# Attention and a gated feed-forward in one kernel: token blocks of 384 become blocks of 512, with a first pass laid out anew

## The chip, the core and the metric

The kernel runs on one NeuronCore of a Trainium2 chip. TensorE (PE in the profile; its weight loads are PEld) multiplies 128x128 stationary weights by a moving operand and adds into PSUM, eight banks of 128 x 2 KB. VectorE (DVE) and ScalarE (ACT) do elementwise work, GpSimd (POOL) a little of it and one DMA queue, SyncE (SP) issues nearly all DMAs. The metric is the device time of one launch in microseconds (us).

## What is computed

```python
# q, k, v: (8, 8, 576, 64) float32
pool = 8
scale = 1.0 / np.sqrt(D)
k_p = k.reshape(B, H, Sp, pool, D).mean(axis=3)
v_p = v.reshape(B, H, Sp, pool, D).mean(axis=3)
scores = scale * np.matmul(q, k_p.transpose(0, 1, 3, 2))
scores = scores - np.max(scores, axis=-1, keepdims=True)
attn = np.exp(scores)
attn = attn / (np.sum(attn, axis=-1, keepdims=True) + 1e-09)
return np.matmul(attn, v_p).astype(np.float32)
...
# x: (4608, 512) from the heads; w_gate, w_val: (512, 1536) float64; w_out: (1536, 512) float64
gate = 1.0 / (1.0 + np.exp(-(x @ w_gate)))
val = x @ w_val
return (gate * val @ w_out).astype(np.float32)
```

Keys and values are averaged in groups of eight, so each query sees 72 keys. The 4,608 rows of `x` are called tokens below. Nearly all multiplications lie in the three products with the weights.

## The kernel before

**Precision.** A float32 operand of the three products is split in a high part, a copy rounded to TensorE's float32r, and a low part, the rest. A product is then three matmuls: high x high, high x low, low x high. ACT writes the high part and DVE subtracts to get the low one (`split`, L173 to 176). The weights arrive as float64 words; `to_f32` (L191) makes float32 of them in four instructions, two on ACT and two on DVE.

**Blocks.** The tokens are cut into `NB` = 12 blocks of `BT` = 384. A matmul of the first two products ("chain") moves 384 columns, one block. A batch has 576 tokens, so a block can touch two batches; `segments` cuts it there.

**Passes.** `first_pass` (L878) takes blocks 0 and 1 plainly: for each of 12 chunks `f` of the hidden width, `whole` (L658) makes gate and value with 12 matmuls each, and `accumulate` (L1153) makes the third product with 128x512 matmuls. Meanwhile it loads and converts every weight (`converted`, `converted_o`, `summed_o`), writes the split parts to DRAM for later (`keep_parts`, `keep_whole`, `keep_o`, `keep_sums`), and does the attention of blocks 0 to 3. Its instructions stand on every engine in the order of the words of `ORDER` (L67): for instance `conv.0.3` is one more step of converting the gate weights of pair 3, `G.1.5` a product, `lw` a load of weights, `acc.4.0` a step of the third product.

Then five passes take two blocks each, with seven products in place of eight by sums of blocks (Winograd's form): `hidden` (L713) walks six pairs `p` of chunks through `SLOTS`, 14 products of 6 matmuls each (`product`, L618; the matmul is L627), and `second_sums` (L809) does the third product with 21 units (m, q) of 12 matmuls (L844). So a pass has 504 + 252 matmuls. Between them one step at a time of the attention of the next pass's blocks is put in (`attention`, L485, a generator; `tasks`). The last pass has none. In the first of the five, pass 1, chunks 10 and 11 go plainly (`hidden_second`, L687: 96 matmuls, L667), and only five pairs follow, whose parts are partly new: `add_up` (L257) makes the sums of the quarters of a weight on DVE, and `reload(..., fresh=True)` splits one part of each group (L175, L176) and stores it from POOL's queue.

**Order.** In the passes a scheduler orders each engine's instructions by estimated due times, apart from those held in program order; engines are in order when they run.

**Rooms in SBUF.** Tags name the rooms: `big` (4 rooms of 8 KB per partition: raw weights, sums, the third product's operands `hs`), `parts` (8 of 4 KB: weight parts of the chain), `oparts` (4 of 4 KB: parts of `w_out`), `xo1` to `xo7` (the split parts of x). In the third product `reload_s` (L364) fetches the parts of unit i+2 and `operand` (L793) splits its `hs` while unit i runs, both into rings of four.

**PSUM.** Six banks `b0` to `b5` hold chains and third products, `sc` and `tp` attention. The scores of a block and a pair of heads are 3 x 144 columns, one bank; `reduce_max` (L506), a subtraction (L509) and one exponential over two pairs (L514) follow. In blocks 0 to 3 the exponential reads PSUM with the maximum as its bias, six instructions of 72 columns (L983). After a product with m = 1, 5 or 6, ACT copies the bank (L633) before the next product may add to it.

## Time and profile before

| | us |
|---|---|
| median of 3 runs (959.38 to 962.64) | 962.57 |
| the profiled execution, its own time | 963.26 |
| its span, first to last instruction | 961.5 |
| first pass, to the last 128x512 matmul of its third product | 215.7 |
| pass 1, to its last third-product matmul | 160.1 |
| passes 2, 3, 4 | 150.7, 150.6, 151.0 |
| pass 5 (no attention beside it) | 129.7 |
| last stores | 3.7 |

The stages are read from the trace by the first and last start of the third product's matmuls (L1159 in the first pass, 252 of L844 in each later one). Busy time of an engine is the union of its instructions; a matmul's recorded duration, 334 ns for 384 columns, holds its way through the array, so the distance from start to start is what one costs in a stream.

### The profile page before, as it was taken

Reading aid. Unit: us, or ns where it says so; the run is one execution under the profiler, and the core shown is the slowest. Engines: PE = TensorE matmul, PEld = TensorE weight load, DVE = VectorE, ACT = ScalarE, POOL = GpSimd, SP = SyncE. Lnnn points to the kernel's source line nnn. Section 1 sums busy time; section 2 is a strip of 40 time slices with the busy share of each in tenths; the row PEclk is TensorE's granted clock in tenths of the full one; section 3 lists DMA queues with packets and bytes.
Section 4 is the critical chain, followed back from the end, with each engine's and each line's share of the span. In section 5 each row is a group of like instructions: output and inputs, shape, how many; then the busy total and the mean of one; then the engine's idle time right before and its main releaser. Section 6 shows DMA issues by size and latency. Waiting matters only on the chain.

```text
span 961.5 us, 15330 instructions
## 1 busy us (share of the span) xinstructions
PE 931.8 (97%) x5400; PEld 901.3 (94%) x5400; DVE 680.7 (71%) x1207; ACT 554.9 (58%) x1142; POOL 70.0 (7%) x107
## 2 busy tenths in 40 slices
PE   4899999999999999999999999999999999999998
PEld 4799998889999999999999999999999999999997
DVE  6987777768888897767586566688476678344483
ACT  6998865544666576656554456655456556233352
POOL 1200000001332100000000000000000000000000
PEclk9999999999999999999999999999999999999999
DMA  9998967779977478988378867568877548877476
GB/s 306 379 294 313 343 228 253 252 257 342 324 259 232 138 238 294 373 312 255 120 226 275 277 228 249 177 200 256 300 254 243 179 121 262 287 233 247 153 221 217
DMA packets 107324, 243.23 MB, mean 253 GB/s; under 512 B 11376, under 2 KB 45936, under 8 KB 105712
## 3 DMA queue, kind: packets, MB, share of 16 engines
q1 hardware_dynamic: 104048, 231.77, 72.6%
q0 software_dynamic: 3200, 10.49, 2.8%
q8 instruction: 43, 0.70, 0.3%
q14 instruction: 33, 0.27, 0.1%
HBM read 191.88 MB, written 50.33 MB: 252 GB/s over the span
## 4 chain that ended last, share of the span: by engine, by line
PE 69%; DMA 7%; DVE 3%; ACT 1%; issue 1%; SPq 0%; DVEq 0%; ACTq 0%
PE chain L627 37%; PE acc L844 21%; PE sc L460 3%; PE chain L667 2%; PE av L469 2%; PE acc L1159 2%; DMA out<-o 1%; DMA raw<-in_kT 1%; PE tp L548 1%; DMA oparts<-keptS 1%; DMA w<-keptwV 1%; DMA raw_o<-in_wo 0%; DMA parts<-keptV2B 0%; DMA oparts<-keptO 0%; DMA parts<-keptV3B 0%
## 5 line engine op out<-in xcount | busy, mean ns | idle before, releaser
L627 PE MATMUL chain<-xo,parts 128*128 128x384 f32 x2436 | 453.7, 338 | 5.7 <-DVE y L639 1.7
L627 PEld LDWEIGHTS chain<-xo,parts 128*128 128x128 f32 x2436 | 419.8, 188 | 10.3 <-issue 2.8
L844 PE MATMUL acc<-hs,oparts 128*128 128x384 f32 x1260 | 227.7, 335 | 1.8 <-ACT hs L803 0.5
L844 PEld LDWEIGHTS acc<-hs,oparts 128*128 128x128 f32 x1260 | 218.3, 188 | 3.6 <-issue 2.3
L639 DVE TENSOR_TENSOR y<-chain,sG 128x384 f32<-128x384 f32 x87 | 48.0, 552 | 67.8 <-ACT sG L633 26.5
L667 PE MATMUL chain<-xo,parts 128*128 128x384 f32 x504 | 93.2, 339 | 0.0
L667 PEld LDWEIGHTS chain<-xo,parts 128*128 128x128 f32 x504 | 88.4, 190 | 0.3
L639 DVE TENSOR_TENSOR y<-chain,sV 128x384 f32<-128x384 f32 x87 | 47.9, 552 | 47.2 <-PE chain L627 32.4
L645 ACT ACTIVATE gate<-y 128x384 f32<-128x384 f32 x87 | 45.6, 525 | 54.4 <-DVE y L639 54.0
L633 ACT COPY sV<-chain 128x384 f32<-128x384 f32 x87 | 41.1, 477 | 53.7 <-PE chain L627 35.9
L803 ACT CAST hs<-h 128x768 fp32r<-128x768 f32 x60 | 50.2, 837 | 32.8 <-PE acc L844 30.2
L633 ACT COPY sG<-chain 128x384 f32<-128x384 f32 x87 | 41.2, 476 | 42.3 <-PE chain L627 42.1
L804 DVE TENSOR_TENSOR hs<-h,hs 128x768 fp32r<-128x768 f32 x60 | 56.7, 953 | 12.4 <-ACT hs L803 12.3
L542 POOL TENSOR_TENSOR pm<-e,rz 128x384 f32<-128x384 f32 x32 | 28.7, 895 | 441.0 <-DVE r L482 223.6
L803 ACT CAST hs<-s 128x768 fp32r<-128x768 f32 x45 | 37.3, 837 | 27.9 <-PE acc L844 19.8
L1159 PE MATMUL acc<-oparts,hs 128*128 128x512 f32 x216 | 51.8, 393 | 0.2 <-DVE hs L1149 0.2
L460 PE MATMUL sc<-kbd,raw 128*128 128x144 f32 (+1 forms) x280 | 47.4, 299 | 3.3 <-DVE r L481 2.8
L648 DVE TENSOR_TENSOR h<-y,gate 128x384 f32<-128x384 f32 x87 | 48.5, 559 | 1.8
L804 DVE TENSOR_TENSOR hs<-s,hs 128x768 fp32r<-128x768 f32 x45 | 43.0, 967 | 8.0 <-ACT hs L803 7.9
L1159 PEld LDWEIGHTS acc<-oparts,hs 128*128 128x128 f32 x216 | 40.2, 188 | 8.7 <-DVE hs L1149 0.8
L460 PEld LDWEIGHTS sc<-kbd,raw 128*128 128x128 f32 (+1 forms) x280 | 37.0, 179 | 10.7 <-issue 4.8
L667 PE MATMUL chain<-xo,parts_x 128*128 128x384 f32 x168 | 31.3, 336 | 1.0 <-DVE h L1140 1.0
(224 smaller groups left out, 1157.5 us busy)
## 6 DMA issues: line engine op xcount, KB each, us to landing
oparts<-keptS SPq DMA_DIRECT2D x60, 512.0 KB, 4.6
oparts<-keptO SPq DMA_DIRECT2D x90, 256.0 KB, 4.2
raw<-in_wgv SPq DMA_DIRECT2D x12, 1024.0 KB, 7.1
raw<-in_qT SPq DMA_DIRECT2D x42, 192.0 KB, 3.8
out<-o SPq DMA_DIRECT2D x40, 192.0 KB, 5.1
raw<-in_kT SPq DMA_DIRECT2D x26, 288.0 KB, 4.5
raw<-in_vm SPq DMA_DIRECT2D x28, 256.0 KB, 4.1
raw_o<-in_wo SPq DMA_DIRECT2D x12, 512.0 KB, 4.7
```

The lines of the kernel that those rows point to most:

```text
L460: nc.tensor.matmul(sc[lo - i * P:hi - i * P, i], lhsT=q[:, lo:hi], rhs=kbd[slot(b, p)], start=True, stop=True)
L542: behind(nc.gpsimd.tensor_tensor(out=pm, in0=e[:, n, :, :KM], in1=rz[:, n, :, None].broadcast_to([P, 2 * QT, KM]), op=ALU.mult), end)
L627: nc.tensor.matmul(t, lhsT=w[:, h, a], rhs=x[:, y, c], start=(m in (1, 2, 5) and c == 0 and k == 0), stop=(c == 1 and k == 2), skip_group_ ...
L633: nc.scalar.copy(s, t)
L639: nc.vector.tensor_tensor(out=y, in0=t, in1=seen[kind, {2: 1, 3: 6, 7: 5}[m]], op=ALU.add)
L645: nc.scalar.activation(gates[q[0]][:, q[1]], y, AF.Sigmoid)
L648: nc.vector.tensor_tensor(out=hb[f // 4][:, f % 4, q[0] * BT:(q[0] + 1) * BT], in0=y, in1=gates[q[0]][:, q[1]], op=ALU.mult)
L667: nc.tensor.matmul(t, lhsT=w[:, c // 2, h, a], rhs=x[:, y, c % 2], start=(c == 0 and k == 0), stop=(c == NC - 1 and k == 2),)
L803: nc.scalar.copy(hs[:, 0], x)
L804: nc.vector.tensor_tensor(out=hs[:, 1], in0=x, in1=hs[:, 0].bitcast(F32), op=ALU.subtract)
L844: nc.tensor.matmul(acc[name, c], lhsT=w[:, k, h, c * P:(c + 1) * P], rhs=hs[:, y, k], start=(m in (1, 2, 5) and i % 3 == 0 and k == 0 and ...
L1159: nc.tensor.matmul(acc[i], lhsT=hss[f][:, y, a], rhs=oparts[f][:, w], start=(f == 0 and k == 0), stop=(f == NF - 1 and k == 2),)
```

## The change

`BT` becomes 512, so there are 9 blocks. Block 0 alone goes plainly in the first pass, which also does the attention of blocks 1 and 2; four passes of two blocks follow (blocks 2n-1 and 2n). `ORDER` is written anew. The rooms change: one `buffer` function names 5 rooms of 8 KB (`s1`, `xo3`, `xo6`, `xo7`, `xo5`), 6 of `parts`, 3 of `oparts`; the tag `big` is gone. The third product's `hs` go to the `xo` rooms as their chain products finish, from the eighth unit on to three of them in turn. Scores of 4 x 144 columns don't fit a bank, so they are made in two halves, in passes both in `sc`. `BIASED` blocks 3 and 4 (whose attention lies in pass 1) take the exponential from PSUM in instructions of 72 columns; the others subtract first. In pass 1 both parts of a group are made anew, from a sum buffer in `hb[1]`, so the first pass doesn't store the parts of chunks 0 to 9. Loads of parts run six groups ahead (`load_next`).

```diff
-BT = 384
+BT = 512
+HT = QT // 2
+BIG = ("s1", "xo3", "xo6", "xo7", "xo5")
+WRING, ORING = 6, 3
+BIASED = (3, 4)
...
-    rawp, big, wpool, opool = sb("rawp", 4), sb("big", 4), sb("wpool", 8), sb("opool", 4)
+    rawp, wpool, opool = sb("rawp", 3), sb("wpool"), sb("opool")
...
+    def buffer(at, shape, dtype, name):
+        if at < 5:
+            return work.tile(shape, dtype, name=name, tag=BIG[at])
+        if at < 5 + WRING:
+            return wpool.tile(shape, dtype, name=name, tag=f"parts{at - 5}")
+        return opool.tile(shape, dtype, name=name, tag=f"oparts{at - 5 - WRING}")
...
+    def otile(shape, dtype, name):
+        turns[0] += 1
+        return buffer(5 + WRING + turns[0] % ORING, shape, dtype, name)
...
+    MADE = {"A": slice(0, 5, 4), "B": slice(3, 7, 3), "C": slice(2, 6, 3), "D": slice(7, 8)}
...
     def reload(kind, p, g, fresh=False):
-        t = wpool.tile([P, 2, 2, HALF], F32R, name="parts", tag="parts")
+        ring.append(ring.pop(0))
+        t = wpool.tile([P, 2, 2, HALF], F32R, name="parts", tag=f"parts{ring[-1]}")
...
+        if fresh:
+            split(t[:, :n, 0], t[:, :n, 1], summed[kind, p][:, MADE[g]])
+            nc.gpsimd.dma_start(outside, inside)
+        else:
+            nc.sync.dma_start(inside, outside)
...
     def reload_s(m, q):
-        t = opool.tile([P, 2, 2, HALF], F32R, name="oparts")
+        t = otile([P, 2, 2, HALF], F32R, "oparts")
...
+            for hf in range(2):
+                sc = room_for([P, HT, 2 * KEYS], "sc")
+                score_matmuls(sc, q, segs, p, hf)
...
+                pinned(nc.vector.reduce_max(out=m, in_=scv, axis=AX.X, negate=j in BIASED))
+                if j in BIASED:
+                    for i in range(QT):
+                        nc.scalar.activation(e[:, n, QT * hf + i], scv[:, i], AF.Exp, bias=m[:, i:i + 1])
+                else:
+                    nc.vector.tensor_tensor(
+                        out=e[:, n, QT * hf:QT * hf + QT], in0=scv, in1=m[:, :, None].broadcast_to([P, QT, KEYS]),
+                        op=ALU.subtract,
+                    )
+                yield
...
-    TURNS = {1: (4, 0, 1, 2, 3), 2: (3, 2, 1, 0, 4, 5), 3: (5, 4, 3, 2, 1, 0), 4: (0, 1, 2, 3, 4, 5), 5: (5, 4, 3, 2, 1, 0)}
+    TURNS = {1: (4, 0, 1, 2, 3), 2: (0, 1, 2, 3, 4, 5), 3: (0, 1, 2, 3, 4, 5), 4: (0, 1, 2, 3, 4, 5)}
...
+    def load_next():
+        if ahead_of:
+            kind, p, g, fresh = ahead_of.pop(0)
+            used.append((kind, p, g, fresh, set(m for m in GROUPS[g] if m != 8)))
+            reload(kind, p, g, fresh)
+
+    def consumed(kind, p, m):
+        next(ms for k, q, _, _, ms in used if (k, q) == (kind, p) and m in ms).discard(m)
+        while used and not used[0][-1]:
+            used.pop(0)
+            load_next()
...
+    ROOMS = (1, 5, 6, 2, 3, 7, 4)
+    def operand(i, m, q, n):
...
-        hs = big.tile([P, 2, 2, BT], F32R, name="hs", tag="big")
+        room = ROOMS[i] if i < 7 else (3, 7, 4)[(i - 7) % 3]
+        hs = work.tile([P, 2, 2, BT], F32R, name="hs", tag=f"xo{room}")
...
-            if i >= 8 and i % 2 == 0:
+            if i in (8, 10, 12, 14, 19, 20):
                 tied[0] = True
                 next(build, None)
```

The plain chain and third product of the first pass keep their form: 12 matmuls for each kind and chunk, 3 for each 128 tokens and chunk, each of 512 columns now.

More of the change, by code (lines that the diff above doesn't have):

```diff
@@ L124 @@
+keeps.5 x.2.3 xhi.2.1 xlo.2.1 out.0@0 out.3 xhi.2.0 st.0 out.1 st.3 out.2 st.1 xlo.2.0 st.2
 """
@@ new lines, in attention_then_ffn, with converted_o, keep_o @@
+    wide_o = {}
+    def converted_o(p, at):
+        raw = raws_o[p]
+        w = wide_o[p] = buffer(at.pop(0), [P, 2, DM], F32, "w_o")
+        yield from to_f32(w.rearrange("p k n -> p (k n)"), raw)
+        t = buffer(at.pop(0), [P, 2, 2, DM], F32R, "oparts")
+        nc.scalar.copy(t[:, :, 0], w)
+        yield
+        nc.vector.tensor_tensor(out=t[:, :, 1], in0=w, in1=t[:, :, 0].bitcast(F32), op=ALU.subtract)
+        oparts[p] = t
+        yield
+    def keep_o(p):
+        for k in range(2):
@@ L749, in hidden @@
             pass
-    def loaded(kind, p, m, left, then, fresh):
-        g, i = place(m)
-        left[kind, p, g] = left.get((kind, p, g), 0) + 1
-        if left[kind, p, g] == sum(m != 8 for m in GROUPS[g]):
-            reload(kind, then, g, fresh)
-    def store(o, r, acc, eng):
-        if eng is nc.vector:
-            nc.vector.tensor_copy(o, acc)
-        else:
-            nc.scalar.copy(o, acc)
-        nc.sync.dma_start(out[r:r + P], o)
     s1 = {}
@@ L1142, in h_of, with accumulate @@
             )
[L1144 to L1154 removed]
+        def accumulate(f):
+            for i in range(QT):
```

612 lines of the change are left out of this document (275 added, 337 removed).

## The prediction

> **What bounds the kernel now.** First I read the profile's first line and its chain of work that ended last, then the busy times of each stage, cut at the ends of the passes (first row: the columns).
>
> ```profile
> span 961.5 us, 15330 instructions
> PE 69%; DMA 7%; DVE 3%; ACT 1%; issue 1%; SPq 0%; DVEq 0%; ACTq 0%
> ```
> ```profile
> core 0: us, PE busy (x) PEld busy (x) DVE busy (x) ACT busy (x) POOL busy (x), PEclk, DMA share, GB/s
> 0.00:20.00 20.00, 8.30 (x40) 6.90 (x40) 12.43 (x26) 11.55 (x39) 3.98 (x21) 1.00 0.87 294
> 20.00:60.00 40.00, 35.54 (x209) 32.57 (x210) 37.11 (x76) 37.75 (x118) 8.75 (x9) 0.91 1.00 357
> 60.00:215.70 155.70, 153.97 (x837) 143.30 (x836) 116.62 (x205) 107.17 (x207) 6.58 (x6) 1.00 0.78 274
> 215.70:375.80 160.10, 157.16 (x947) 154.26 (x946) 137.15 (x264) 101.28 (x210) 30.87 (x50) 1.00 0.76 258
> 375.80:526.50 150.70, 150.15 (x886) 146.17 (x885) 106.40 (x186) 83.19 (x169) 5.16 (x6) 1.00 0.80 264
> 526.50:677.10 150.60, 148.31 (x872) 145.84 (x871) 102.92 (x178) 82.96 (x160) 7.04 (x8) 1.00 0.72 235
> 677.10:828.10 151.00, 150.87 (x894) 147.01 (x893) 102.25 (x178) 82.59 (x159) 7.60 (x8) 1.00 0.70 227
> 828.10:957.80 129.70, 127.47 (x727) 125.22 (x725) 65.77 (x99) 47.91 (x86) 0.00 (x0) 1.00 0.71 227
> ```
>
> From 60 us on PE is busy 97 to 100% of every stage, and nothing else comes near. Before that it isn't: between 20 and 60 us the DMA engines are full (1.00 at 357 GB/s), DVE and ACT at 93 and 94%. So the change has to be judged in two places: what a matmul costs where PE rules, and whether PE still rules in a first pass that has less for it to do.
>
> **What a matmul costs.** Two stretches of the timeline of PE, 384 columns and 512 (start, length, count):
>
> ```profile
> 836.91 45.34 PE L627 MATMUL chain<-xo,parts 128*128 128x384 f32 x260 [0.81 <-ACT sV L633]
> ```
> ```profile
> 205.38 4.27 PE L1159 MATMUL acc<-oparts,hs 128*128 128x512 f32 x18
> 209.49 1.23 PE L667 MATMUL chain<-xo,parts_x 128*128 128x384 f32 x6
> ```
>
> 260 matmuls take 45.34 us with the last one's way through the array (0.34), so 45.0/259 = 174 ns each. 18 of 512 columns take 209.49 - 205.38 = 4.11 us, 228 ns each. The difference, 54 ns for 128 columns, is 0.42 ns a column; the part that doesn't grow is about 13 ns, and it is paid for fewer, wider matmuls. The Trainium skill, "TensorE: Matmul & The Clock Gate", section "Wait — 56ns, not 53.3ns?", gives a back-to-back gap of N / 2.4 GHz + about 2.5 ns; by that figure 1,116 matmuls fewer would save 2.8 us in fixed cost, not 14.5, and the whole would come out some 12 us later than below. The rows measure both widths, and they decide.
>
> **The passes, step by step.** The groups of instructions give the counts:
>
> ```profile
> L627 PE MATMUL chain<-xo,parts 128*128 128x384 f32 x2436 | 453.7, 338 | 5.7 <-DVE y L639 1.7
> L844 PE MATMUL acc<-hs,oparts 128*128 128x384 f32 x1260 | 227.7, 335 | 1.8 <-ACT hs L803 0.5
> L667 PE MATMUL chain<-xo,parts 128*128 128x384 f32 x504 | 93.2, 339 | 0.0
> L667 PE MATMUL chain<-xo,parts_x 128*128 128x384 f32 x168 | 31.3, 336 | 1.0 <-DVE h L1140 1.0
> L1159 PE MATMUL acc<-oparts,hs 128*128 128x512 f32 x216 | 51.8, 393 | 0.2 <-DVE hs L1149 0.2
> ```
>
> Before, 4,368 of 384 and 216 of 512. After, 23 pairs x 84 = 1,932 in chains, 4 x 252 = 1,008 in third products, 96 plain in pass 1; first pass 288 + 144: 3,468, all of 512. In time: 4,368 x 0.174 + 216 x 0.228 = 809.3, against 3,468 x 0.228 = 790.7. **If PE ruled throughout, the change is worth 18.6 us.** It isn't spread evenly: the first pass loses 576 x 0.174 + 216 x 0.228 - 432 x 0.228 = 51.0 us of PE work, and the passes gain 32.
>
> A pass of 756 matmuls costs 756 x 0.174 = 131.5 us; passes 2 to 4 took 19.3 us more, pass 5, without attention, 1.8 less. So attention on PE costs 19.3 us for 768 tokens; its matmuls follow the tokens (the splits at batches stay as many), so 25.7 for 1,024. Pass 1 holds 768 matmuls, of which some 11 (six of them in the row above) already ran beside the first pass: 757 x 0.174 = 131.7, attention 19.3, and 9.1 us of stalls of its own.
>
> After: pass 1 757 x 0.228 + 25.7 + stalls of 12 (9.1 scaled by the longer pass) = 210.3; passes 2 and 3 172.4 + 25.7 = 198.1 each; pass 4 172.4 - 1.8 = 170.6; last stores 3.7. Sum **780.8**, against 745.8 before.
>
> DVE in pass 1 must not take over. Durations by size:
>
> ```profile
> L1140 DVE TENSOR_TENSOR h<-chain,y 128x384 f32<-128x384 f32 x24 | 13.0, 549 | 5.2 <-PE chain L667 5.1
> L1149 DVE TENSOR_TENSOR hs<-h,hs 128x768 fp32r<-128x768 f32 x12 | 11.3, 953 | 0.8 <-ACT hs L1146 0.7
> L348 DVE TENSOR_TENSOR sums<-raw_o,sums 128x1024 fp32r<-128x1024 f32 x6 | 7.3, 1221 | 1.6 <-ACT sums L346 1.6
> L176 DVE TENSOR_TENSOR parts<-w,parts 128x256 fp32r<-128x256 f32 x40 | 17.3, 442 | 0.9 <-ACT parts L175 0.7
> L245 DVE TENSOR_TENSOR parts_x<-w,parts_x 128x512 fp32r<-128x512 f32 x6 | 4.1, 687 | 5.0 <-ACT parts_x L243 5.0
> ```
>
> A chain result goes from 0.55 to about 0.69 (50 of them, +7), a third operand or sum from 0.953 to 1.221 (some 50, +13); the weight splits become 30 of 0.687 and 10 of 0.442 in place of 40 of 0.442 (+7); a second batch of keys and values adds about 9. DVE goes from 137 to some 174 us of 210: 83%, before 86%. So no new bound there, and the stalls scale. The stores of these parts from POOL's queue carry twice the data; what waits behind them on POOL is the attention's `pm`, which has a whole pass of cover.
>
> The third product's rings shrink from four to three, so the fetch of unit i+2 starts when unit i-1 ends and has two units, 2 x 12 x 0.228 = 5.5 us.
>
> ```profile
> L373 SPq DMA_DIRECT2D oparts<-keptS x60: 319/320/522, 220.2 to 948.0; - x60
> ...
> DMA to landing us min/median/max: 3.1/4.6/7.3
> ```
>
> The median lands in time, the slowest 1.8 us late. From below 0, from above 84 units x 1.8 = 151 us; I take 2, near the median.
>
> **The first pass.** PE work falls to 197.8 - 51 = 147 us (8.30 + 35.54 + 153.97 are the 197.8), so it can't be the only bound. DVE had 166.2. It loses 12: `h` 24 x 0.549 to 12 x 0.69, `hs` 12 x 0.953 to 6 x 1.221, the split of x 8 of 768 to 4 of 1,024 and 4 of 512, the rest by fewer and wider instructions; 154 remain. ACT, 156.5 before, loses in the same places. DMA: the rows of the first three stages sum to 62.8 MB. The stores of parts of chunks 0 to 9 go (30 like the two below):
>
> ```profile
> keptG0C<-parts SPq DMA_DIRECT2D x1, 256.0 KB, 5.2
> ```
> ```profile
> keptV4C<-parts_x SPq DMA_DIRECT2D x1, 256.0 KB, 6.1
> ```
>
> 30 x 256 KB = 7.9 MB, and 0.5 of output: 54 MB remain, at 357 GB/s 152 us. So PE 147, DVE 154, DMA 152, ACT somewhat below its 156: **four resources within some 10 us of each other, where PE alone used to rule.** How full can a stretch run in which all compete? The row of 20 to 60 us shows it: DVE 93%, ACT 94%, DMA 100%, PE 89%. With the first 20 us as they were: 20 + (154 - 12.4)/0.93 = **172 us** (before 215.7). Bounds: 215.7 - 51 = 165 if PE keeps its fill, 20 + 141.6/0.85 = 187 if DVE fills to 85% only.
>
> **Sum.** 172 + 780.8 + 2 = 954.8 us of span against 961.5. The profiled execution's own time is 1.8 above its span (963.3), so 956.6; that execution was 0.7 above the median, so **956**, 0.7% less.
>
> **The rivals.**
>
> *PE still rules the first pass.* Then it ends at 165 and the time is 949. For it: from 60 us PE filled 99%. Against: DVE's 154 and DMA's 152 don't leave 165 much room. Chance 0.12.
>
> *Four engines in turn.* Each instruction is fixed in its engine's order, and a conversion crosses ACT and DVE several times; with none of them far ahead, every late DMA stops several. DVE filled to 88% gives 181, and 965: no change. For it: between 60 and 215 us DVE and ACT never ran over 75%; against: the row of 20 to 60 us. Chance 0.24.
>
> *Slower: exponentials on ACT in pass 1.* Blocks 3 and 4 take theirs in 16 groups of four small instructions between the gates' sigmoids. The rows of pass 1 before, and of a small exponential:
>
> ```profile
> L514 ACT ACT_TABLE_LOAD x4 | 5.1, 1283 | 0.7 <-DVE e L509 0.6
> L645 ACT ACT_TABLE_LOAD x4 | 5.1, 1283 | 0.1
> ```
> ```profile
> L983 ACT ACTIVATE e<-sc,small 128x72 f32<-128x72 f32 x48 | 10.9, 351 | 0.2
> ```
>
> A group holds ACT for 1.28 + 4 x 0.35 = 2.7 us, and the next sigmoid loads its table again. The copy that frees a bank (L633) has two products, 12 x 0.228 = 2.7 us, before PE needs it. If each group makes one copy 1 us late, that is 16 us on PE: 972. It decides once a copy waits over 2.7 us. Against: the passes before hide a whole exponential and its two loads, and four groups could share a load. The Trainium skill, "ScalarE: Activation LUTs", section "What ACT_TABLE_LOAD costs", counts 1.28 us for the load and 1.38 more for a drain, which would make a group 4.1 us and this rival certain; the rows show 0.7 us of idle time before four loads, so I leave the drain out. Chance 0.18.
>
> *The third product waits for its weights.* If a unit in ten is 1 us late, 8 us: 963, no change. Chance 0.06. The forecast keeps 0.40.
>
> **Chances.** About 0.5% is what a measurement can tell from no change: faster means under 957.8, slower over 967.4. Faster: PE's rival 0.12, three quarters of the forecast's 0.40, a few hundredths of the rest: 0.45. Slower: the exponentials 0.18, a third of the case of four engines: 0.25. Same: 0.30. The range is 940 (first pass 165, no stalls in pass 1) to 975 (first pass 187 and a few us in the passes); the likeliest case alone has 950 to 963.
>
> **What would show it.** Chain and third product at 228 ns from start to start; passes 2 and 3 near 198 us; the first pass's last 128x512 matmul near 172 us with DVE over 90% busy from 20 us on. Wrong would be PE idle before L627 by ACT in pass 1, L844 waiting for `oparts`, or PE busy in less than 80% of the first pass.

## The result, and the profile after

| | before | after |
|---|---|---|
| median, us | 962.3 | 973.5 |
| range of the runs, us | 959.4 to 962.6 | 971.2 to 976.7 |
| the profiled execution, its span, us | 961.5 | 970.3 |

The changed kernel is 1.3% slower: the ratio is 1.0126, with a 95% interval of 1.0088 to 1.0164. The forecast was 956 us, 0.7% faster. Between the spans of the profiled executions the miss is 970.3 - 954.8 = 15.5 us.

The first two lines below are the page's first line and its chain of work that ended last, of the kernel after; then its busy times by stage, cut at the ends of the passes.

```profile
span 970.3 us, 12391 instructions
PE 75%; DVE 5%; DMA 3%; ACT 2%; issue 1%; DVEq 0%; ACTq 0%
```
```profile
core 0: us, PE busy (x) PEld busy (x) DVE busy (x) ACT busy (x) POOL busy (x), PEclk, DMA share, GB/s
0.00:20.00 20.00, 10.78 (x51) 9.97 (x52) 7.50 (x14) 9.57 (x34) 2.53 (x19) 1.00 0.92 332
20.00:60.00 40.00, 32.37 (x152) 25.04 (x152) 38.55 (x71) 37.02 (x83) 4.71 (x4) 0.91 0.89 311
60.00:172.30 112.30, 107.17 (x526) 86.74 (x525) 106.51 (x172) 97.68 (x194) 11.62 (x8) 1.00 0.88 316
172.30:384.70 212.40, 205.45 (x962) 164.15 (x962) 162.68 (x266) 152.21 (x293) 31.60 (x48) 1.00 0.63 215
384.70:596.20 211.50, 203.60 (x956) 164.93 (x955) 147.91 (x222) 112.80 (x191) 11.07 (x8) 1.00 0.67 218
596.20:794.30 198.10, 195.62 (x909) 158.92 (x908) 131.59 (x194) 98.81 (x156) 8.61 (x8) 1.00 0.60 193
794.30:966.60 172.30, 171.67 (x738) 137.72 (x737) 84.97 (x101) 61.91 (x88) 0.00 (x0) 1.00 0.57 183
```

Each row holds one stage of the forecast, so they can be set side by side:

| stage | forecast, us | measured, us |
|---|---|---|
| first pass | 172 | 172.3 |
| pass 1 | 210.3 | 212.4 |
| **pass 2** | **198.1** | **211.5** |
| pass 3 | 198.1 | 198.1 |
| pass 4 | 170.6 | 172.3 |
| last stores | 3.7 | 3.7 |
| third product's weights | 2 | in the passes above |

Pass 2 alone is 13.4 us over, and that is nearly the whole miss, although its forecast is the same as that of pass 3. Two things make it longer than pass 3. PE is idle for 7.9 us of it (211.50 less 203.60) against 2.5, and it holds more work: 956 matmuls against 909, 8.0 us more of PE. Counted in the trace by their starts, 25 more of them are chain matmuls (517 against 492): a pass begins its chain beside the third product of the pass before, as far as its `x` is built, and pass 2 could begin less of it than pass 3. 24 more multiply with the values (72 against 48), eight of them the end of block 4's attention, and four fewer make scores. The longest waits of PE from 384 to 597 us (who waited for whom, us in total, times, the longest):

```profile
PE chain L618 <- DVE xo L159: 3.3, 4, 1.5
PE chain L618 <- ACT kbd L401: 1.7, 1, 1.7
PE chain L618 <- ACT xo L158: 1.3, 1, 1.3
```

The same from the timeline of PE (start, length, the group, and in brackets the idle time before it):

```profile
389.66 0.73 PE L618 MATMUL chain<-xo,parts 128*128 128x512 f32 x2 [1.28 <-ACT xo L158]
391.58 3.08 PE L618 MATMUL chain<-xo,parts 128*128 128x512 f32 x12 [1.19 <-DVE xo L159]
396.11 4.68 PE L618 MATMUL chain<-xo,parts 128*128 128x512 f32 x18 [1.45 <-DVE xo L159]
...
416.63 2.76 PE L618 MATMUL chain<-xo,parts 128*128 128x512 f32 x11 [1.70 <-ACT kbd L401]
```

PE starts pass 2 and stops again and again, because `xo`, the split parts of x, aren't built. They can't be: they are sums of blocks 3 and 4, and ACT copies the last piece of block 4 out of the attention only now. The copies of x in pass 1, all eight of them before, and then the last four after, which are block 4's (count, duration, first and last start):

```profile
L559 ACT COPY xs<-av x8: 456/476/485, 262.0 to 349.3; 128x384 f32<-128x384 f32 x8
```
```profile
L550 ACT COPY xs<-av x4: 564/566/588, 337.5 to 386.3; 128x512 f32<-128x512 f32 x4
```

Before, the last copy started 26 us ahead of the end of pass 1 (375.8). After, it starts at 386.3, 1.6 us behind the end of pass 1 (384.7). The attention of blocks 3 and 4 has taken all of pass 1 and has become what the next pass waits for. PE is busy 97% of pass 1, so neither the shares nor the waits inside that pass show it: the price stands in the next stage, as a wait and as work that came too late for pass 1.

### The profile page after: what moved, and what is told of

Same layout as the page of the kernel before. It is cut to its first block, busy times and chain, and to the rows that moved or that the text cites. A ratio compares the mean times of both kernels' runs of the same rounds, so it can differ in the third digit from the quotient of the medians.

```text
span 970.3 us, 12391 instructions
## 1 busy us (share of the span) xinstructions
PE 926.7 (96%) x4284; PEld 747.5 (77%) x4284; DVE 679.7 (70%) x1036; ACT 570.6 (59%) x1037; POOL 70.1 (7%) x95
## 4 chain that ended last, share of the span: by engine, by line
PE 75%; DVE 5%; DMA 3%; ACT 2%; issue 1%; DVEq 0%; ACTq 0%
PE chain L618 41%; PE acc L836 23%; PE chain L658 3%; PE av L461 3%; PE sc L452 2%; PE acc L1150 1%; DMA oparts<-keptS 1%; PE tp L539 1%; DMA h<-keptwV 1%; DMA parts<-keptG1B 1%; DMA raw<-in_kT 1%; DVE y L630 0%; DVE xo L159 0%; DVE hs L796 0%; DVE s L587 0%
## 5 line engine op out<-in xcount | busy, mean ns | idle before, releaser
L618 PE MATMUL chain<-xo,parts 128*128 128x512 f32 x1932 | 471.7, 397 | 14.1 <-DVE xo L159 3.3
L618 PEld LDWEIGHTS chain<-xo,parts 128*128 128x128 f32 x1932 | 356.2, 188 | 100.8 <-DVE xo L159 4.8
L836 PE MATMUL acc<-hs,oparts 128*128 128x512 f32 x1008 | 244.6, 396 | 2.3 <-DMA oparts<-keptS 1.7
L630 DVE TENSOR_TENSOR y<-chain,sG 128x512 f32<-128x512 f32 x69 | 47.5, 689 | 71.8 <-ACT sG L624 34.3
L658 PE MATMUL chain<-xo,parts 128*128 128x512 f32 x384 | 92.2, 395 | 2.1 <-DVE parts L226 0.8
L658 PEld LDWEIGHTS chain<-xo,parts 128*128 128x128 f32 x384 | 71.0, 188 | 19.5 <-DVE parts L226 2.2
L796 DVE TENSOR_TENSOR hs<-h,hs 128x1024 fp32r<-128x1024 f32 x48 | 59.0, 1230 | 34.3 <-ACT hs L795 34.2
L795 ACT CAST hs<-h 128x1024 fp32r<-128x1024 f32 x48 | 50.4, 1050 | 51.1 <-PE acc L836 45.0
L636 ACT ACTIVATE gate<-y 128x512 f32<-128x512 f32 x69 | 43.6, 632 | 44.7 <-DVE y L630 44.3
L796 DVE TENSOR_TENSOR hs<-s,hs 128x1024 fp32r<-128x1024 f32 x36 | 45.1, 1253 | 16.7 <-ACT hs L795 16.6
L630 DVE TENSOR_TENSOR y<-chain,sV 128x512 f32<-128x512 f32 x69 | 46.8, 684 | 8.2 <-PE chain L618 5.1
L639 DVE TENSOR_TENSOR h<-y,gate 128x512 f32<-128x512 f32 x69 | 46.9, 688 | 0.8
L639 DVE TENSOR_TENSOR h<-chain,gate 128x512 f32<-128x512 f32 x23 | 15.9, 690 | 26.5 <-PE chain L618 26.3
```

What stands on the lines that cost most here:

```text
L618: nc.tensor.matmul(t, lhsT=w[:, h, a], rhs=x[:, y, c], start=(m in (1, 2, 5) and c == 0 and k == 0), stop=(c == 1 and k == 2), skip_group_ ...
L630: nc.vector.tensor_tensor(out=y, in0=t, in1=seen[kind, {2: 1, 3: 6, 7: 5}[m]], op=ALU.add)
L636: nc.scalar.activation(gates[q[0]][:, q[1]], y, AF.Sigmoid)
L639: nc.vector.tensor_tensor(out=hb[f // 4][:, f % 4, q[0] * BT:(q[0] + 1) * BT], in0=y, in1=gates[q[0]][:, q[1]], op=ALU.mult)
L658: nc.tensor.matmul(t, lhsT=w[:, c // 2, h, a], rhs=x[:, y, c % 2], start=(c == 0 and k == 0), stop=(c == NC - 1 and k == 2),)
L795: nc.scalar.copy(hs[:, 0], x)
```

## The experiments

The first theory (A): the first products of pass 2 wait because block 4's attention is late, and it is late for want of room on DVE. The rivals: the exponentials on ACT (rival C, the slower one of the prediction), the wider matmul itself, and pass 2's own loads. All times below come from the traces; "last copy" is the end of the last copy of x's pieces in pass 1, from the start of the span.

| run | pass 1 | pass 2 | last copy | end of pass 2 minus last copy | median, us |
|---|---|---|---|---|---|
| the changed kernel | 212.4 | 211.5 | 386.9 | 209.3 | 973.5 |
| e1 early attention | 216.1 | 211.3 | 390.5 | 209.2 | 973.9 |
| e2 sums on POOL | 215.1 | 201.8 | 378.5 | 210.9 | 964.8 |
| e3 subtraction on DVE | 203.8 | 223.8 | 387.4 | 211.1 | 974.4 |
| e4 parts kept | 207.3 | 210.9 | 390.8 | 208.8 | 976.0 |
| e5 = e2 and e3 | 210.0 | 211.5 | 384.0 | 209.1 | 967.6 |
| e6 = e5 and e1 | 209.2 | 211.9 | 383.8 | 209.6 | 965.6 |
| e10 sums on POOL, block 3 subtracts | 207.3 | 209.1 | 375.9 | 212.7 | 963.4 |
| e11 sums on POOL, in order | 204.6 | 218.9 | 386.8 | 206.3 | 973.3 |
| e12 more sums on POOL | 213.8 | 202.4 | 376.1 | 211.8 | 968.2 |
| e13 more on DVE | 212.8 | 211.3 | 385.5 | 209.2 | 969.2 |
| e14 more on ACT | 214.2 | 212.2 | 387.5 | 210.0 | 972.1 |
| e15 second room for pm | 211.2 | 210.8 | 384.5 | 208.5 | 968.1 |
| e16 = e15 and e3 | 207.9 | 216.2 | 382.6 | 211.3 | 970.0 |
| e17 = e15 and e10 | 211.4 | 213.3 | 384.4 | 210.4 | 969.7 |
| e9 late half left out | 214.1 | 198.3 | | | 957.6 (one time) |
| e18 one score tile a pair | 215.6 | 196.1 | 328.7 | 253.5 | 962.1 |

The fifth column is the finding that all runs together gave. In the first fifteen rows pass 1 goes from 203.8 to 216.1 and pass 2 from 201.8 to 223.8, but **pass 2 ends 206 to 213 us after the last copy of x**, wherever pass 1 ended. Only where the copy comes early (e9, e18) does pass 2 end by PE's work, 196 to 198 us after pass 1.

**e1: the attention's steps earlier in pass 1.**

```diff
-                if n == 1 and i in (1, 3, 5, 7, 9, 11, 13) or n > 1 and (i % 3 == 2 or i == 7 or p == 0):
+                if n == 1 and i in (0, 1, 3, 4, 6, 7, 9, 10, 12) or n > 1 and (i % 3 == 2 or i == 7 or p == 0):
```

> Pass 1 takes the attention's steps at nine products of a pair instead of seven, so that block 4's attention is finished before the third product begins. Theory A (the first product of pass 2 waits because block 4's attention ends after the third product of pass 1, so that the last sums of x come late): the last copy of x in pass 1 ends well before 384 us, PE's waits for xo at the start of pass 2 (now about 8 us) vanish, pass 2 falls from 211.5 to about 202 us; pass 1 stays within 212 to 218, since the same work is only moved; the whole is 964 to 970. Theory B (pass 2 is long because its 512-column matmuls take longer than 228 ns and because of its own waits): pass 2 stays over 209 and the whole at 972 to 976.

973.9 us (ratio to before 1.009, 1.0056 to 1.0124), and the last copy came 3.6 us later, not earlier. Where the steps are written doesn't decide when they run: a scheduler orders them. Nothing follows on theory A but that this was no way to move the copy.

**e2: the sums of `add_up` on POOL.**

```diff
-        in_turn(nc.vector.tensor_tensor(out=w[:, 4:6], in0=w[:, 1:3], in1=w[:, 0:2], op=ALU.subtract))
-        nc.vector.tensor_tensor(out=w[:, 6], in0=w[:, 2], in1=w[:, 4], op=ALU.subtract)
-        nc.vector.tensor_tensor(out=w[:, 7], in0=w[:, 3], in1=w[:, 6], op=ALU.subtract)
+        in_turn(nc.gpsimd.tensor_tensor(out=w[:, 4:6], in0=w[:, 1:3], in1=w[:, 0:2], op=ALU.subtract))
+        nc.gpsimd.tensor_tensor(out=w[:, 6], in0=w[:, 2], in1=w[:, 4], op=ALU.subtract)
+        nc.gpsimd.tensor_tensor(out=w[:, 7], in0=w[:, 3], in1=w[:, 6], op=ALU.subtract)
```

> The three subtractions of add_up go from DVE to POOL, about 13.8 us of DVE's 162.7 in pass 1. Theory A1 (DVE's backlog in pass 1 is what makes the attention of block 4, and with it x's parts, late): the last copy of x in pass 1 comes some 10 us earlier, pass 2 falls to about 204 and the whole to about 966. Theory A2 (the place of the steps, not DVE's load, makes them late): the last copy of x stays at 384 to 387 and pass 2 over 209; or the slower POOL makes the weight's sums late and pass 1 grows.

The two passes of e2 in its busy times by stage (columns as above):

```profile
172.60:387.60 215.00, 206.91 (x975) 166.25 (x973) 162.87 (x241) 158.44 (x300) 59.88 (x74) 1.00 0.62 213
387.60:589.40 201.80, 199.84 (x943) 163.90 (x943) 142.47 (x217) 109.81 (x187) 11.46 (x8) 1.00 0.71 229
```

964.8 us (1.0022, 1.0 to 1.0043): 9 us better than the changed kernel. The copy came 8 us earlier and pass 2 fell by 9.7, near A1's numbers. But DVE (the third of the busy times) was as busy in pass 1 as without the edit, 162.87 against 162.68 us. The 15 us that went to POOL came back: some of DVE's instructions took longer beside it (last section), and the first combines of pass 2's x fell into this stage. So the gain is real, and DVE's busy time in pass 1 does not explain it.

**e3: no small exponentials on ACT.**

```diff
-BIASED = (3, 4)
+BIASED = ()
```

> Blocks 3 and 4 subtract the maximum on DVE and take one exponential over two pairs, as the others do: 64 small exponentials (about 22 us of ACT) become 4 large ones, and DVE gets 16 subtractions of about 0.45 us (7 us). Rival C of the prediction (small exponentials on ACT hold up the bank's copies in pass 1): pass 1 falls from 212.4 by some us and the whole goes below 970. Theory A1 (DVE's backlog): the last copy of x comes some 7 us later, PE waits longer at the start of pass 2, and the whole is 973 to 982.

```profile
170.90:374.70 203.80, 200.39 (x937) 162.60 (x936) 165.28 (x272) 116.36 (x205) 29.97 (x47) 1.00 0.65 223
374.70:598.50 223.80, 212.52 (x982) 172.97 (x980) 153.29 (x231) 116.19 (x200) 11.72 (x9) 0.95 0.64 207
```

Busy times by stage of e3: ACT lost 36 us in pass 1 (152.2 to 116.4), pass 1 became 8.6 us shorter, and the whole did not (974.4; 1.0111, 1.0086 to 1.0136): pass 2 grew by 12.3. The last copy still came at 387. So rival C has half a point: the small exponentials do hold PE up in pass 1. Yet they are not what the time was lost to, since the gain only became a longer wait for x. This is the clearest sign that PE's work didn't set the end of these two stages.

**e4: the parts of chunks 0 to 9 kept again.** The first pass stores them (`keep` words in `ORDER`), pass 1 loads all but one of a group:

```diff
-            split(t[:, :n, 0], t[:, :n, 1], summed[kind, p][:, MADE[g]])
-            nc.gpsimd.dma_start(outside, inside)
+            i = n - 1
+            if i:
+                nc.sync.dma_start(inside[:, :i], outside[:, :i])
+            split(t[:, i, 0], t[:, i, 1], summed[kind, p][:, SUM[g]])
+            nc.gpsimd.dma_start(outside[:, i], inside[:, i])
```

> The first pass stores the parts of chunks 0 to 9 again (30 stores of 256 KB, 7.9 MB), and pass 1 loads them and splits one part of a group anew, as in the kernel before: about 7 us less on DVE and 7 less on ACT in pass 1. If DMA bounds the first pass (54 MB in 172 us, 0.88 to 0.92 busy): it ends at 190 to 195 instead of 172.3. If DVE bounds it, it ends at 172 to 178. Theory A1: pass 2 falls by up to 7 us. Whole: about 990 by the first, about 970 by the second.

The first pass of e4, whole:

```profile
0.00:181.30 181.30, 151.82 (x723) 122.68 (x724) 153.59 (x255) 144.42 (x309) 18.89 (x31) 0.96 0.96 346
```

It ended at 181.3, between the two expectations: 7.9 MB more cost 9.0 us, with the DMA engines 96% busy at 346 GB/s. So DVE's order (95% busy after 20 us, in the kernel after) and DMA lie that close together in the first pass. Pass 1 won 5 us, pass 2 nothing, and the whole was 976.0 (1.0124, 1.0097 to 1.0152).

**e5 and e6: both engines relieved.** e5 is e2 and e3 together, e6 adds e1's steps.

> Both edits together: the sums of add_up on POOL, and the maximum of blocks 3 and 4 subtracted on DVE with one exponential over two pairs. Theory F (two engines, not one, are overfull in pass 1: ACT by the small exponentials, which cost pass 1 some 9 us, and DVE by the weight's sums, which cost the start of pass 2 some 10 us; each edit alone only shifts the load to the other): pass 1 about 204 to 206, pass 2 about 200 to 204, the whole 952 to 958, faster than both kernels. Theory G (either edit's gain is the same gain, or POOL's slower sums hold up the weights): the whole 964 or more.

> As the run before it, with the attention's steps of pass 1 at nine products of a pair instead of seven. If with both engines relieved the place of the steps decides when block 4's attention ends: its last copy of x falls from 378 to below 370 us, pass 2 to 198 to 200, the whole 950 to 956. If the engines' order still decides: the last copy stays within 3 us, and the whole too.

967.6 (1.004, 1.0018 to 1.0062) and 965.6 (1.0021, 0.9993 to 1.0049). Theory F fell: the gains of e2 and e3 don't add, and the last copy went back from 378 to 384.

**e7 and e8: the matmul's width alone.** In each chain product five matmuls of six move fewer columns.

```diff
+                e = BT if c == 0 and k == 0 else 496
                 nc.tensor.matmul(
-                    t, lhsT=w[:, h, a], rhs=x[:, y, c],
+                    t[:, :e], lhsT=w[:, h, a], rhs=x[:, y, c, :e],
```

> Leaves out columns: after the first of each chain product, its matmuls move 496 columns instead of 512. It measures the distance from start to start alone. If a matmul costs 13 ns and 0.42 ns a column, evenly: 221 ns in each, with the spread of the 384-column ones (173 to 174). If the spread of 224 to 241 at 512 columns comes from the full width of a bank: 221 ns flat here. If it comes from something that goes with the weight loads or the moving operand at any width near this: 217 to 234 here too, with a mean near 224.

> Leaves out columns: the same with 448 columns. 201 ns flat if 13 ns + 0.42 ns a column holds; a spread of some 17 ns and a mean near 204 if the unevenness goes with any width over 384; and if the wider matmuls only stall at the turn from one weight to the next, the spread falls with the width.

One execution of each took 954.8 and 943.8 us, with columns left out; they measure the distance alone.

Long unbroken stretches of the timeline of PE in the last pass, of the changed kernel, of e7 and of e8 (a group that mixes widths is named by one of them):

```profile
808.69 96.66 PE L618 MATMUL chain<-xo,parts 128*128 128x512 f32 x417
```
```profile
794.75 93.89 PE L619 MATMUL chain<-xo,parts 128*128 128x496 f32 x417
```
```profile
790.04 84.17 PE L619 MATMUL chain<-xo,parts 128*128 128x512 f32 x402 [1.18 <-DMA parts<-keptG1A]
```

With the last matmul's 0.40 us taken off: 96.26/416 = 231.4 ns from start to start at 512 columns. In e7 the mean is 224.7; a sixth of its matmuls are of 512, so those of 496 cost (6 x 224.7 - 231.4)/5 = 223.4. In e8, 208.9, so 204.4 for 448. From 384 columns (174 ns in the kernel before) the prediction's 0.42 ns a column leads to 200.9, 221.0 and 227.8. All three wider ones lie 2 to 4 ns above. So it is not the full bank: each width measured over 384 costs this, and in these stretches nearly all single distances at 512 lie between 224 and 238 ns and those at 448 between 195 and 214, where those of 384 are 173 or 174. What causes it stays open.

**e9: the late half left out.** For block 4's second group of heads, keys and values are prepared, the rest is replaced by copies:

```diff
+        if (j, g) == (4, 1):
...
+                nc.scalar.copy(xs[side(j)][:, p], xs[side(j)][:, p - 2])
+                yield
+            return
```

> Leaves out scores, exponential and the product with the values for block 4's second group of heads (keys and values are still prepared; x's third and fourth part are copies of its first two), the piece that ends last in pass 1. Theory A (this lateness is what makes pass 2 13 us too long): the combine of x's parts runs 15 us or more before the end of pass 1, PE's waits for xo at the start of pass 2 vanish, pass 2 is 198 to 200. Pass 1 loses the piece's own 6.4 us on PE (a quarter of 25.7): 204 to 206. Whole 953 to 957. Theory B (pass 2 has a cause of its own, as its loads of parts or the preparation of keys): pass 2 stays over 205.

Passes 1 and 2 of e9:

```profile
170.70:384.90 214.20, 207.10 (x949) 164.74 (x948) 168.37 (x269) 152.61 (x281) 35.20 (x47) 0.99 0.63 217
384.90:583.20 198.30, 196.76 (x924) 160.90 (x923) 138.34 (x207) 104.74 (x180) 9.16 (x8) 1.00 0.68 226
```

The first combine of x's parts ran at 349 us, and pass 2 took 198.3, as theory A said and theory B did not. **The lateness of block 4's attention is the cause of pass 2's 13 us.** Pass 1 did not become shorter, against the expectation (214.1, PE's waits up to 375 us add up to 7 us there), although e9 leaves out work, estimated at 6.4 us on PE. So the two passes together gained 11.5 us (412.4 against 423.9), and part of that is the work left out.

**e10, e11: the load shared more finely, and the order.** e10 is e2 with `BIASED = (4,)`; e11 is e2 with DVE's maxima and sums of keys and values kept in program order in pass 1 (`steady[0] = True`).

> The sums of add_up on POOL, and only block 3 subtracts on DVE; block 4 keeps its small exponentials. With the sums on POOL, ACT was busy 108 of the 128 us up to 300 us, and PE waited 5.7 us for small exponentials, 3.5 of it before 300 us, in block 3 and the start of block 4. If the load of each engine decides: pass 1 about 211, pass 2 stays 202, the whole about 961. If the order of the instructions decides, which every edit changes: pass 2 goes back to 209 to 212 and the whole stays at 965 to 970.

> The sums of add_up on POOL, and in pass 1 the attention's maxima and the sums of keys and values are kept in program order on DVE, as they are in the later passes. If the place of block 4's attention in DVE's order decides when it ends: the last copy of x comes before 365 us (378 with the sums on POOL alone), pass 2 is 198 to 200, the whole 960 to 963. If pass 1 is simply too full, DVE's weight splits come later instead: pass 1 grows by as much, the whole 965 or more.

963.4 (1.0003, 0.9982 to 1.0023): the best of the whole study that computes everything, and no better than the kernel before. e11: 973.3 (1.0122, 1.0098 to 1.0145), pass 1 short, the copy late, pass 2 long, as in e3.

**e12, e13, e14: load taken away and added.** e12 is e10 with the sums of the hidden parts (`minus`) on POOL in pass 1. e13 and e14 are the changed kernel with work for nothing behind each `add_up`, six subtractions on DVE or, in the same place, six times `nc.scalar.copy(extra, x)` on ACT:

```diff
+        for i in range(6):
+            x = w[:, 4 + i // 2, P * (i & 1):P * (i & 1) + P]
+            nc.vector.tensor_tensor(out=extra, in0=x, in1=x, op=ALU.subtract)
```

> As the run with the sums on POOL and block 3 subtracting on DVE, and in pass 1 the sums of the hidden parts for the third product (12 of 128x1024, 1.22 us each on DVE) go to POOL as well: 14.7 us more off DVE, most of it at the end of pass 1. So far passes 1 and 2 together took 423.9 us in the changed kernel, 416.9 with 13.8 us off DVE, 418.2 with 7.4 off it, and 427.6 with 7 more on it, about half a us for each us on DVE. Theory H (it is DVE's work in pass 1 that is paid, in pass 1 or at the start of pass 2): passes 1 and 2 fall from 416.4 to about 409, the whole from 963.4 to about 956, faster than before. Theory I (POOL, at 2.7 us for such a sum, makes the operands of the third product late): the third product waits and the whole stays at 963 or goes above.

> The changed kernel, with six subtractions of 128x128 more on DVE after each add_up, whose result nobody uses: 60 x about 0.29 us, 17 us more on DVE in pass 1, and nothing else. Theory H: passes 1 and 2 together go from 423.9 to about 432, the whole to about 982. If DVE's load is not what is paid: within 3 us of 973.5.

> The same on ACT: 60 copies of 128x128 more, 20 us or more of ACT in pass 1. Theory H: the whole within 3 us of 973.5, since taking 22 us of exponentials off ACT did not shorten passes 1 and 2 together. Theory J (both engines are equally overfull, so that any work on either is paid): passes 1 and 2 together grow by 8 us or more, as with DVE.

Pass 1 of e13 and of e14:

```profile
170.70:383.50 212.80, 207.42 (x962) 166.85 (x961) 178.25 (x326) 152.20 (x294) 31.22 (x48) 0.98 0.62 213
```
```profile
171.20:385.30 214.10, 206.88 (x962) 165.44 (x961) 162.67 (x266) 164.17 (x353) 31.50 (x48) 0.99 0.63 213
```

DVE really had 15.6 us more (178.25 against 162.68) and ACT 12 (164.17 against 152.21). Neither moved the copy (385.5 and 387.5), and the wholes were 969.2 (1.0063, 1.004 to 1.0086) and 972.1 (1.0102, 1.0057 to 1.0147): no slower than the changed kernel. e12, with still less on DVE, had its copy at 376.1 where e10 had 375.9, and was slower (968.2; 1.0041, 1.0022 to 1.006), with the time that theory I had. **Theory H, and with it the second half of theory A, fell: the copy doesn't follow the busy time of DVE or ACT.** What e13 and e14 add has no consumer, though, and may stand where the engine is idle, so a load that stands in the way of the attention's own steps isn't ruled out.

**e15, e16, e17: one link of the chain loosened.** If not load, then a chain of steps that wait for each other. Its links can be read from rows. POOL's `pm` in pass 1 (busy, mean ns, then its idle time by releaser):

```profile
L533 POOL TENSOR_TENSOR pm<-e,rz 128x512 f32<-128x512 f32 x8 | 9.8, 1230 | 62.6 <-DVE r L474 42.9 <-PE tp L539 19.7
```

Of eight `pm`, three waited 19.7 us in all for PE to transpose the one before, since `pm` has one room; and the next group's exponentials wait for the second `pm` to have read `e`. e15 puts the second `pm` in a room of the raw loads:

```diff
-            pm = work.tile([P, 2 * QT, KM], F32, name="pm")
+            if n and j < 5:
+                pm = rawp.tile([P, S], F32, name="raw")[:, :BT].rearrange("p (i k) -> p i k", k=KM)
+            else:
+                pm = work.tile([P, 2 * QT, KM], F32, name="pm")
```

e16 adds e3's edit, e17 e10's.

> The changed kernel, but in blocks 3 and 4 the second pair's pm of each group gets a room of the raw loads' ring instead of waiting for the first pair's. Theory K (the attention of pass 1 is one serial chain through single rooms: a group's first exponential waits until the second pm of the group before has read e, and that pm waits until the first has been transposed, 19.7 us of waits on POOL in pass 1): e is free some 7 to 9 us earlier in each of three groups, the last copy of x falls from 387 to about 365, PE's waits for xo at the start of pass 2 vanish, pass 2 is 198 to 202, the whole 960 to 966. Theory L (the places in the engines' queues, as the scheduler estimated them, decide): the last copy stays within 5 us of 387 and the whole at 970 to 976.

> The second room for pm, and blocks 3 and 4 subtract on DVE with one exponential over two pairs. Subtraction alone gave pass 1 203.8 and pass 2 223.8 us, because x's parts came as late as before. Theory K: with e free earlier the last copy falls to about 365 to 370 here too; pass 1 about 204, pass 2 200 to 205, the whole 948 to 956, faster than both kernels. Theory L: 967 to 975.

> The second room for pm, the sums of add_up on POOL, and block 3 subtracting on DVE (without the room: pass 1 207.3, pass 2 209.1, the last copy of x at 376, the whole 963.4). Theory K: the last copy at about 358, pass 2 198 to 201, the whole 952 to 956. Theory L: 962 to 968.

968.1 (1.0045, 1.0025 to 1.0065), 970.0 (1.0081, 1.0049 to 1.0112) and 969.7 (1.007, 1.0045 to 1.0094). Theory K fell in its numbers: the copy moved from 386.9 to 384.5, where theory L had it, though the times fit L in e16 alone (970 to 976, 967 to 975 and 962 to 968 were expected by it). The rows show where the link went. The last group in the changed kernel (timelines of POOL and of PE):

```profile
360.32 1.04 POOL L533 TENSOR_TENSOR pm<-e,rz 128x512 f32<-128x512 f32 x1 [30.51 <-DVE r L474]
371.50 1.04 POOL L533 TENSOR_TENSOR pm<-e,rz 128x512 f32<-128x512 f32 x1 [10.14 <-PE tp L539]
```
```profile
370.73 0.60 PE L539 MATMUL tp<-cst,pm 128*128 128x128 f32 x4
...
381.09 0.60 PE L539 MATMUL tp<-cst,pm 128*128 128x128 f32 x4
```

and in e15:

```profile
359.89 1.04 POOL L536 TENSOR_TENSOR raw<-e,rz 128x512 f32<-128x512 f32 x1
```
```profile
367.71 0.60 PE L542 MATMUL tp<-cst,pm 128*128 128x128 f32 x4
...
378.58 0.60 PE L542 MATMUL tp<-cst,raw 128*128 128x128 f32 x4
```

In the changed kernel the first `pm` is done at 361.4 and is transposed at 370.7; the second is done at 372.5 and is transposed at 381.1. Some 18 of the last 26.5 us are such gaps, while PE is never idle (54.7 of 54.7 us from 330 on): the transposes stand in PE's order among the third product's matmuls, and the bank `tp` must be read out before it is written again. In e15 the second `pm` is done 11.6 us earlier, at 360.9, and its transposes still run at 378.6. The first pair's transposes and its product hold the same bank until its copy ends at 374.3, and PE then has 23 matmuls of the third product in its order (373.2 to 378.6) before them. One wait was taken away, and the next links took nearly all of it.

**e18: fewer hops.** What the change did to this chain is to halve the score tiles: a pair has two turns of score matmul, maximum and exponential through the bank `sc` in place of one. e18 takes the second turn out in blocks 3 and 4, and lets its exponentials read the first half's scores:

```diff
             for hf in range(2):
+                if not hf or j not in BIASED:
                     sc = room_for([P, HT, 2 * KEYS], "sc")
...
```

> Leaves out the scores and maxima of the second half of each pair in blocks 3 and 4: the exponentials of both halves read the first half's scores, in one go (their number stays). So a pair has one score tile, as in the kernel before, and the attention's chain in pass 1 loses eight of sixteen turns of score matmul, maximum and exponential through the bank sc. The engines lose little: 3.6 us on DVE, 3 on PE. Theory M (the chain is long because each hop waits for its place in an engine's order, and halving the scores doubled the hops): the last copy of x falls from 387 to 365 or earlier, pass 2 is 198 to 202, pass 1 204 to 212, the whole 950 to 960. Theory L (the estimated places decide, whatever the chain): the last copy stays at 382 to 388 and pass 2 at 209 or more, the whole 966 to 973.

The copies of x (the last four of these eight belong to block 4) and the stages of pass 1 and pass 2:

```profile
L551 ACT COPY xs<-av x8: 563/566/591, 220.0 to 328.2; 128x512 f32<-128x512 f32 x8
```
```profile
170.50:386.10 215.60, 207.94 (x980) 167.35 (x979) 175.35 (x279) 151.31 (x304) 36.67 (x50) 1.00 0.65 219
386.10:582.20 196.10, 194.60 (x905) 158.63 (x904) 136.30 (x201) 100.98 (x171) 7.26 (x6) 1.00 0.70 227
```

The last copy came at 328.7, 58 us earlier, although the engines have hardly less to do (ACT 151.3 us in pass 1 as in the changed kernel, DVE more, since block 5's attention now begins there; what is left out was put at 3.6 us on DVE and 3 on PE). The lead grows along the chain: the eight copies start 14, 11, 28, 30, 53, 53, 63 and 58 us earlier than in the changed kernel, with two turns less for every two of them, so a turn cost some 7 us. PE waited 1.5 us in the first 54 us of pass 2, none of it for `xo`. Pass 2 took 196.1 and the whole 962.1 (ratio to before 0.9988, 0.9964 to 1.0011); passes 1 and 2 together fell from 423.9 to 411.7. Theory M holds for the copy and for pass 2: **the number of hops decided, each with its wait for a place in an engine's order and for a room.** How much of a hop is place and how much is room, no run separates. Pass 1 did not fall as M expected (215.6, not 204 to 212), since part of pass 2's work moved into it, and the whole came out above its 950 to 960.

## Why the prediction was wrong

**The step that failed** is the one on pass 1 of the part "The passes, step by step". It worked out DVE's busy time there and ended "So no new bound there, and the stalls scale", and it said of the attention's `pm` that it "has a whole pass of cover". The busy time was near (174 us forecast, 162.7 measured), and in e13 15.6 us more of it did no harm. What the step left out is the attention as a chain. The forecast has the halved scores only as 16 groups of small instructions on ACT, in a rival, and nowhere as hops: eight more waits in a row. Before, the chain ended 26 us ahead of the pass; after, 2 us behind it, and pass 2 (forecast 198.1) paid 13.4. e9 and e18, in which the copy is early, give 198.3 and 196.1 for that pass. None of the three signs of being wrong that the prediction named came (PE was busy 87% of the first pass, and neither ACT in pass 1 nor the weights of the third product held it up for long); what failed stood at a place that it did not watch.

**How much of the miss that is.** Less than the 13.4 us. With the copy early, pass 1 is longer (214.1 and 215.6 against 212.4, forecast 210.3), because more of the next pass runs in it. Passes 1 and 2 together gain 11.5 us in e9 and 12.2 in e18, and of these some 6 and 3 are work left out. So the lateness cost the whole some 5 to 9 of the 15.5 us, by this estimate. The rest lies in the same two passes, which with the copy early and work left out still take 411.7 and 412.4 us, where 408.4 was forecast. Some 5 us of it are the wider matmuls (the mis-sized term below, 1,513 of them); what the others are is not shown.

**Right by their working, with some luck.** The first pass: 172 forecast, 172.3 measured; DVE 154 forecast and 152.6 measured (7.50 + 38.55 + 106.51), 95% busy after 20 us where 93% was taken; PE 147 forecast, 150.3 measured; 54 MB forecast and some 54.6 moved (GB/s times length of the three rows). Four resources do lie close together, and e4 prices one of them: 7.9 MB, 9.0 us. That it came out to 0.3 us is luck: less of DVE's work fell into the first 20 us than was taken (7.5 against 12.4 us), and the higher fill afterwards made up for it. The last stores were right. The third product's waits for its weights: 2 us taken, 1.7 measured on the page:

```profile
L836 PE MATMUL acc<-hs,oparts 128*128 128x512 f32 x1008 | 244.6, 396 | 2.3 <-DMA oparts<-keptS 1.7
```

**A term that was mis-sized.** 228 ns for a matmul of 512 columns came from 18 matmuls; 416 give 231.4. That is 756 x 3.4 ns = 2.6 us a pass. In pass 3 it can't be seen, since its window holds only 744 of these matmuls (492 and 252): 12 more of them ran ahead, in pass 2, than it ran ahead of pass 4. 198.1 - 744 x 0.2314 = 25.9 us remain for attention and stalls, where 25.7 was forecast. So the 198.1 of pass 3 is exact by luck, two misses of the same size. Pass 4, with no attention, took 1.7 us more than forecast. The Trainium skill, "TensorE: Matmul & The Clock Gate", section "Wait — 56ns, not 53.3ns?", has N / 2.4 GHz + about 2.5 ns, by which an estimate is 216 ns at 512 columns and 162.5 at 384. The widths measured here lie 12 (384) to 16 ns (512) above that, so the trace doesn't agree here.

**The rivals.** PE did not rule the first pass (165 us, forecast at 0.12). Four engines in turn (181): no. The exponentials on ACT gave 972, which is where the time came out, but by another mechanism: e3 takes them away without a gain in the whole, e18 keeps them without a loss, and 12 us more on ACT (e14) cost nothing. A time that fits is no proof of its cause. The third product's weights: no.

**Still open.** Why moving 30 sums to POOL brought the copy 8 us forward (e2) while 60 subtractions more on DVE didn't push it back (e13): those have no consumer and may stand where DVE is idle, but that was not tried. Up to the sixth copy e2 was 22 us ahead of the changed kernel, and at the eighth only 8, so what takes the lead back lies in the last group. Nor does any run have x early and no small exponentials: e3's pass 1 (203.8) says that they hold PE up, and what they would cost then isn't known. Edits that should be neutral moved the whole by up to 4 us (e13), through the order, as it seems. No version that computes everything beat the kernel before.

## What to carry to other kernels

Before a tile is cut in two to fit a room, follow the chain that runs through that room and count its hops: on full in-order engines a hop costs some us of waiting, however short its instruction is, and no busy share shows it. For each stage, ask not only which engine is fullest but when the thing that the next stage starts with is ready, and how many us of slack it has: here 26 us of slack were what the change used up. And where an edit shortens one stage and lengthens the next by as much, a clock common to both is running: look for the event from which the end of the second has a constant distance.

## What the runs showed of the hardware

A pause at PE can cost more than its length. In e3 PE does little between the end of pass 1 (374.7) and 390 us, and at 399.6 it waits for a load; the matmuls behind each of the two run at 427 ns instead of 231. The second wait, and the granted clock of both stretches (the column behind POOL's):

```profile
404.06 6.49 PE L618 MATMUL chain<-xo,parts 128*128 128x512 f32 x17 [4.46 <-DMA parts<-keptV0C]
```
```profile
390.00:396.00 6.00, 4.88 (x12) 3.42 (x13) 5.79 (x7) 3.97 (x4) 0.00 (x0) 0.55 0.63 210
...
404.00:410.00 6.00, 5.94 (x16) 4.72 (x17) 1.82 (x2) 1.52 (x2) 0.00 (x0) 0.57 0.48 191
```

The trace has the clock at 0.50 from 381.8 to 395.4 us and from 402.3 to 409.1. About 5 us of chain matmuls run at it each time, and some 4 us are lost by them in all. In the changed kernel, whose waits at that place are 1.2 to 1.7 us with matmuls between them, it stays at 1.00 in the row of pass 2.
The Trainium skill, "TensorE: Matmul & The Clock Gate", section "What's actually happening", has the clock at half speed after an idle window of about 3.4 us, until a busy one has passed. The second stretch agrees in the main, with a wait of 4.5 us, 2.7 us into which the clock fell, and 427 ns a matmul, and so do the shorter waits of the changed kernel. The first doesn't: the clock fell at 381.8 with no wait over 1.6 us since the end of pass 1, PE being busy 2.0 of the 3.4 us before.

DVE's instructions got longer beside POOL. Three sums of x (L573), of the same form, in the changed kernel and in e2, where POOL makes the weight's sums at the same time (busy, mean ns):

```profile
L573 DVE TENSOR_TENSOR s<-xs,xs 128x1024 f32<-128x1024 f32 x1 | 1.2, 1224 | 0.0
```
```profile
L573 DVE TENSOR_TENSOR s<-xs,xs 128x1024 f32<-128x1024 f32 x1 | 1.8, 1752 | 0.0
...
L573 DVE TENSOR_TENSOR s<-xs,s 128x1024 f32<-128x1024 f32 x1 | 1.2, 1209 | 0.0
```

1.22 us in the changed kernel, 1.75 beside POOL (185.6 us, with POOL at work from 185.0 to 187.9), and 1.21 for the third line, of e2 while POOL did nothing. The 27 splits of 128x512 went from 0.68 to 0.77 us in the mean. So work moved to POOL is not all taken off DVE.
